# Two loads per chunk of the spectrum instead of three, and a result stored in eight pieces

## The chip, the cores and the metric

The kernel runs on one core of a Trainium2 chip. The metric is the device time of one execution in microseconds (us). A core has a matrix engine (TensorE, PE in the profile, with PEld for its weight loads), three engines for element-wise work (VectorE or DVE, ScalarE or ACT, GpSimd or POOL) and a queue that issues only transfers (SyncE, SP). Transfers (DMAs) can be issued by SP, ScalarE and GpSimd; each tells that it is done through a semaphore. On-chip memory has 128 partitions; matmul results go to a separate memory, PSUM.

## The reference

First a long causal convolution by Fourier transforms, then a mixing over tokens and channels. Batch 8, sequence 5696, 128 channels.

```python
def _attn_ref(x, h):
    B, S, D = x.shape
    L = 2 * S
    Xf = np.fft.rfft(x, n=L, axis=1)
    Hf = np.fft.rfft(h, n=L, axis=0)
    Yf = Xf * Hf[None, :, :]
    y = np.fft.irfft(Yf, n=L, axis=1)[:, :S, :]
    return y.astype(np.float32)

def _moe_ref(x, w_theta, w_tok_r, w_tok_i, w_ch):
    theta = x @ w_theta
    cos_t, sin_t = (np.cos(theta), np.sin(theta))
    zr = x * cos_t
    zi = x * sin_t
    yr = np.einsum('ts,bsd->btd', w_tok_r, zr)
    yi = np.einsum('ts,bsd->btd', w_tok_i, zi)
    y = yr + yi
    u = x + y
    return (u + np.maximum(u @ w_ch, 0.0)).astype(np.float32)
```

The x of the second function is the result of the first.

## The kernel before

**The convolution**, the first 430 us, works in eight groups: two batch rows times one half of the channels (64). The Fourier transform of length 11392 = 178 x 64 is split into matmuls. Stage A (`stage_a`, L248) transforms over the first factor and copies the result to SBUF. Stage B (`stage_b`) goes through the 90 frequencies in 12 chunks of 8 (the last has 2): TensorE does the second factor (`f2`, L268), ScalarE copies the result from PSUM to a tile xs (L417, two buffers), and VectorE multiplies it with the spectrum of h (L419, for the short last chunk L424 twice) into a large tile uv_t. Stage C (L439, L440) and stage D (L475) transform back; stage D's copies (L479, L481) fill a tile yt, 128 partitions (64 channels, two batch rows) by 5696 tokens, of which there is one buffer. PSUM has four buffers that all of these share.

**The spectrum of h** is made once at the start with the same stages (`h_chunk`), its real part in partitions 0 to 63 and its imaginary part in 64 to 127. Its 12 chunks are gathered in the tiles `hst`, which lie in the memory of uv_t, and after every third chunk SP stores three of them to DRAM (`hf_hbm`, L362). The first product of stage B writes over that memory, so it comes after the last of these stores has read it.

In stage B the spectrum comes back chunk by chunk into tiles hs: [128 partitions, 2, 512] in 16 bit, 256 KB. Slot 0 of the middle dimension is the chunk as it lies in DRAM; slot 1 is the same with the two halves of 64 partitions exchanged. L408 loads slot 0, and L410 loads slot 1 in two pieces. There are four buffers hs (`LEAD = 4`): the loads of chunks 0 to 3 are issued during stage C of the group before, and that of chunk c + 4 right after the product of chunk c in the program, so that it waits until that product has freed the buffer.

**The result** of a group is stored to DRAM (`yt_hbm`) by two transfers on SP, one per batch row, 64 partitions by 5696 tokens (L488). For the last group a part goes another way and the rest is issued by GpSimd. The phase steps behind (`phase_step`) read it back, transpose it, take sine and cosine, and store y (L743) and z (L607) on SP; after group 6 SP also copies a part of yt within the chip (L713).

**Order.** The stages of neighbouring groups are woven by hand (`woven`): stage C of group g with stage A of group g + 1, then stage B of group g + 1 with stage D of group g. Below, stage B of "group g" means the products of that group. On TensorE and SP the framework's scheduler sets the order from there. SP takes its queue strictly in that order; an issue that waits holds everything behind it. SP's transfers use eight completion semaphores in turn, and an issue waits until the transfer that used its semaphore before has landed.

**The mixing**, from 430 us on, streams two 5696 x 5696 matrices through TensorE by Strassen-like products (L1266), with GpSimd issuing their loads (L667).

Of the kernel before, what the change touches and what calls it, by code (L numbers as in the profile page):

```python
# [11 lines left out]
BF16 = mybir.dt.bfloat16  # L12
F16 = mybir.dt.float16
# [9 lines left out]
def kernel(  # L23
# [10 lines left out]
    nc = tc.nc  # L34
    B, S, D = x.shape
    assert D == 128
    P = 128
# [28 lines left out]
    H = 22 * P  # L66
# [9 lines left out]
    N2 = 64  # L76
# [3 lines left out]
    CK = 8  # L80
    HD = D // 2
# [6 lines left out]
    NCK = len(CHK)  # L88
    CN = 10
    CHN = [(c0, min(CN, N2 - c0)) for c0 in range(0, N2, CN)]  # L90
    UVW = 2 * HD * K1
    NP = 14
    ND = N2 - 2 * NP
    RC = 2 * NP + 2 * ND
    M0, N0 = S // 4 // N2, S // 4 % N2
    assert S % 4 == 0 and S // 2 == NB // 2 * N2 + N2 // 2 and 2 * NP < N2 // 2
    hf_hbm = nc.dram_tensor("hf_hbm", (NCK, 2, P, HD * CK), F16, kind="Internal").ap()
    yt_hbm = nc.dram_tensor("yt_hbm", (D, B, S), BF16, kind="Internal").ap()

    psp = ExitStack()  # L100
# [2 lines left out]
    def psum():  # L103
        return fp.tile([P, 2, 512], F32, tag="ps", name="ps")

    conv, setup, xa, xin, pha = (ExitStack() for _ in range(5))

    def pool(name, bufs, stack, **kw):
        return stack.enter_context(tc.tile_pool(name=name, bufs=bufs, **kw))

    fa = pool("fft_a", 1, xa)
    fh = pool("fft_h", 4, xa)
    fx = pool("fft_x", 2, xin)
    NE, WB, BT = 9, 6 * 4 * CJ * 64, 7 * 1024
    keep = pool("keep", 1, ctx, side="right")
# [4 lines left out]

    uv_t = fc.tile([P, 2 * UVW + P], F16)
    u_t, v_t = uv_t[:, :UVW + P], uv_t[:, UVW:]
    uv = uv_t[:, :2 * UVW].rearrange("p (r e d k) -> p (r e) d k", r=2, e=2, k=K1)
    a_0 = s1.tile([P, 2 * K1, HD], F16, name="a_0")
# [224 lines left out]
    def h_chunk(c):  # L349
        c0, ck = CHK[c]  # L350
        ps = f2(a_h, c, 0)
        h_ = hst[c // 6][:, c % 6]
        dst = h_[:, :, :, :ck]
        if c in (0, 2, 5, 7, 10):
            nc.vector.tensor_scalar(dst, ps, 16.0 / NF, None, op0=mult)
        else:
            nc.scalar.activation(dst, ps, AF.Copy, scale=16.0 / NF)
        for cc, j in ((0, 0), (NCK - 1, CHK[-1][1] - 1)):
            if c == cc:
                nc.vector.tensor_scalar(dst[:, :, :, j], dst[:, :, :, j], 0.5, None, op0=mult)  # L360
        if c % 3 == 2:
            nc.sync.dma_start(  # L362
                hf_hbm[c - 2:c + 1].rearrange("c h p n -> p (c h) n"),
                hst[c // 6][:, c % 6 - 2:c % 6 + 1].rearrange("p c h d k -> p (c h) (d k)"))

    r_u = fc.tile([P, P], F16)
    r_v = fc.tile([P, RC], F16)
# [27 lines left out]
    def e_minus():  # L395
        nc.gpsimd.tensor_scalar(e_neg[:K1], e_t[:K1, 1:2 * NP:2], -1.0, None, op0=mult)

    LEAD = 4

    def stage_b(a_st, dh, warm=WARM):  # L400

        hs_of = {}

        def load(c):
            if c >= NCK:
                return
            hs = hs_of[c] = fh.tile([P, 2, HD * CK], F16, tag="hs", name="hs")
            nc.sync.dma_start(hs[:, 0], hf_hbm[c, dh])  # L408
            for e in range(2):
                nc.sync.dma_start(hs[64 * e:64 * e + 64, 1], hf_hbm[c, dh, 64 - 64 * e:128 - 64 * e])  # L410

        def chunk(c):
            c0, ck = CHK[c]
            hv = hs_of[c].rearrange("p r (d k) -> p r d k", k=CK)
            ps = f2(a_st, c, warm)
            xs = fs.tile([P, 2, HD, CK], F16, tag="xs", name="xs")
            nc.scalar.activation(xs[:, :, :, :ck], ps, AF.Copy)  # L417
            if ck == CK:
                nc.vector.tensor_tensor(  # L419
                    uv[:, :, :, c0:c0 + ck],  # L420
                    xs.rearrange("p e d k -> p e (d k)").unsqueeze(1).to_broadcast([P, 2, 2, HD * CK]),
                    hv.rearrange("p r d k -> p r (d k)").unsqueeze(2).to_broadcast([P, 2, 2, HD * CK]), op=mult)
            for r in range(2 if ck < CK else 0):
                nc.vector.tensor_tensor(  # L424
                    uv[:, 2 * r:2 * r + 2, :, c0:c0 + ck], xs[:, :, :, :ck],
                    hv[:, r:r + 1, :, :ck].to_broadcast([P, 2, HD, ck]), op=mult)
            load(c + LEAD)
        return [lambda c=c: load(c) for c in range(LEAD)], [lambda c=c: chunk(c) for c in range(NCK)]

# [34 lines left out]
    def stage_d(st, bp, dh, then=None):  # L464
        def chunk(n0, cn):
            if n0 == 0:
                st["yt"] = fy.tile([P, NB, N2], BF16, tag="yt", name="yt")
            g_, yt = st["g"], st["yt"]
            ps = psum()
            nq = 5 if cn == CN else cn  # L470
            for j in range(cn):
                o = ps[:, j // nq, (j % nq) * NB:(j % nq + 1) * NB]
                terms = terms_of(n0 + j)
                for i, (at, e_) in enumerate(terms):
                    nc.tensor.matmul(o, g_[:K1, at, :], e_, start=(i == 0), stop=(i == len(terms) - 1))  # L475
            y_out = yt[:, :, n0:n0 + cn].rearrange("p m (a q) -> p m a q", q=nq)
            y_in = ps[:, :cn // nq, :nq * NB].rearrange("p a (q m) -> p m a q", q=nq)
            if n0 in (0, 3 * CN):
                nc.vector.tensor_copy(y_out, y_in)  # L479
            else:  # L480
                nc.scalar.activation(y_out, y_in, AF.Copy)  # L481
            if n0 + cn == N2:
                if then is not None:
                    then(yt)
                for e in range(2):
                    t0 = H if then else 0
                    with tc.issue_after(sides["row"]) if then else ExitStack():
                        (nc.gpsimd if then else nc.sync).dma_start(  # L488
                            yt_hbm[dh * HD:(dh + 1) * HD, 2 * bp + e, t0:],
                            yt[64 * e:64 * e + 64].rearrange("p m n -> p (m n)")[:, t0:])  # L490
        return [lambda n0=n0, cn=cn: chunk(n0, cn) for n0, cn in CHN]

    zz_n, ZB = [0], 3
# [11 lines left out]
    rr = []  # L505
    r_rest = [lambda: rr.extend([r_table(0, r_u), r_table(1, r_v)]), lambda: rr[0](), lambda: rr[1]()]
    h_chunk(0)
    w2_sine()
    w_rest(1)
    h_chunk(1)  # L510
    w2_cosine()
    for c in range(2, NCK):
        if c == 5:
            w_rest(2)
        h_chunk(c)
        if c in (9, 10):
            a0.pop(0)()
# [19 lines left out]
    def phases_b(ti, y_ap, b0, nb, yT, sb, th_pool, th_tag, zi_eng, turns=None, tags=("red", "mag"), m=P,  # L537
                 theta_ps=None, copy=None, home={}):
        n = nb * D
# [39 lines left out]
        nc.scalar.activation(cos_, mag, AF.Sin, bias=half_pi[:m], scale=-TWO_PI)  # L579
        yflat = y_ap.rearrange("p b d -> p (b d)")  # L580
        if tags is None:
            k = zz_n[0] = (zz_n[0] + 1) % (4 + ZB)
            zz = (fh.tile([P, 2, HD * CK], F16, tag="hs", name="zz").bitcast(BF16) if k < 4 else
                  sides["phases"]["zz"].tile([P, 2, 512], BF16, tag="zz", name="zz"))
            zr, zi = zz[:, 0], zz[:, 1]
            sides["zz"] = zz
        else:
            zi, zr = (z.bitcast(BF16) for z in (sin_, cos_))
# [85 lines left out]
    sides = {"phases": None}  # L674
# [173 lines left out]
    bp = cp = wlp = ybp = None  # L848
# [248 lines left out]
    for i, (k, p, tt, j0, s0, nj) in enumerate(stretches):  # L1097
# [38 lines left out]
        if tt is None:  # L1136
# [24 lines left out]
            if end_of_pair:  # L1161
# [5 lines left out]
                c, c0 = c_last  # L1167
# [161 lines left out]
```

## Time and profile before

| | |
|---|---|
| median of 3 runs | 2084.01 us (2083.17 to 2089.09) |
| the profiled execution | 2084.83 us, span 2083.0 us, mean granted clock 0.978 |
| busy: PE, DVE, ACT, POOL | 1982.1, 1543.9, 639.5, 972.4 us |
| hs loads (SP) | 96 of 128 KB (median 3.1 us to landing), 192 of 64 KB (3.0) |
| spectrum stores (SP) | 4 of 768 KB, 9.0 us |
| result stores (SP) | 14 of 712 KB, 7.7 us; GpSimd 2 of 360 KB |
| first to last start of L419 | 53.2 to 375.1 us |

A row of the groups of instructions reads: line, engine, operation, output <- inputs, shape, count | busy us, mean ns of one | idle us of the engine just before them, and what ended most of it. A row of waits reads: who <- whom: us in total, times, longest. A row of the timeline reads: start us, length us, engine, line, operation, output <- input, count, and in brackets the idle time before it with what ended it. On SP, the length of an issue includes a wait on one semaphore. A row of transfers: count, KB each, median us from issue to landing.

### The profile page before, as it was taken

What the parts mean: (1) busy time and instruction counts of PE and PEld (TensorE: products, weight loads), DVE (VectorE), ACT (ScalarE), POOL (GpSimd) and SP (SyncE); (2) the same over time, 40 slices, a digit from 0 to 9 for tenths busy, and PEclk for the clock granted to TensorE, in tenths of its full rate; (3) what the DMA queues carried; (4) which work ended last, traced back from release to release, by engine and by line L of the source; (5) the groups of instructions that cost most, each with busy time, mean ns of one, the idle gap of its engine ahead of it and who ended that gap; (6) DMA issues with size and microseconds to landing.
All of it is one profiled execution on the core that took longest, in us unless ns stands there. A gap on an engine that the chain in (4) does not pass through costs nothing.

```text
span 2083.0 us, 42942 instructions
## 1 busy us (share of the span) xinstructions
PE 1982.1 (95%) x16381; PEld 1098.0 (53%) x16381; DVE 1543.9 (74%) x2805; ACT 639.5 (31%) x936; POOL 972.4 (47%) x1770
## 2 busy tenths in 40 slices
PE   7698988889999999999999999899999999999998
PEld 5588888754444444444444444344444444444444
DVE  7867767666788787878777766876867777777767
ACT  6667777783333333333310000011111111111111
POOL 8432331247444454445566554445453545444450
PEclk9789999999999999999999999999999999999999
DMA  9699996999898999999999899879697878878793
GB/s 162 97 140 146 157 143 161 240 266 244 147 172 173 178 172 164 175 178 172 179 168 161 131 196 263 132 118 156 119 160 127 154 133 148 144 135 153 129 155 88
DMA packets 518014, 335.08 MB, mean 161 GB/s; under 512 B 186231, under 2 KB 483319, under 8 KB 516823
## 3 DMA queue, kind: packets, MB, share of 16 engines
q0 software_dynamic: 322368, 157.47, 60.0%
q1 hardware_dynamic: 189456, 163.34, 27.7%
q10 hardware_dynamic: 5984, 11.54, 1.6%
q8 instruction: 128, 2.10, 0.4%
q14 instruction: 78, 0.64, 0.1%
HBM read 376.39 MB, written 92.49 MB: 225 GB/s over the span
## 4 chain that ended last, share of the span: by engine, by line
PE 65%; DVE 3%; DMA 3%; issue 1%; POOL 1%; ACT 0%; DVEq 0%; ACTq 0%; SPq 0%
PE m L1266 60%; DVE b L822 1%; DVE c L1273 1%; DMA ring<-in_moe_w_tok_r_dram 1%; PE v L968 1%; PE utp L961 1%; PE m L1270 1%; DMA b<-z_hbm 1%; DVE wt L881 1%; POOL ring L667 1%; PE theta_ps L551 0%; PE tpz L909 0%; DMA wl<-in_moe_w_tok_i_dram 0%; PE m L1187 0%; PE m L1153 0%
## 5 line engine op out<-in xcount | busy, mean ns | idle before, releaser
L667 POOL DMA_DIRECT2D ring<-in_moe_w_tok_i_dram x720 | 387.9, 546 | 651.4 <-DVE wt L881 576.1
L667 POOL DMA_DIRECT2D ring<-in_moe_w_tok_r_dram x720 | 386.5, 547 | 151.0 <-DVE wt L881 82.7
L881 DVE STREAM_TRANSPOSE wt<-ring 128x384 f32<-128x384 f32 (+2 forms) x720 | 360.4, 527 | 120.1 <-PE m L1266 77.5
L1266 PE MATMUL m<-b,wt 128*128 128x512 bf16 x1640 | 390.1, 380 | 1.9 <-DVE wt L881 1.7
L1266 PEld LDWEIGHTS <-wt 128*128 128x128 bf16 x1804 | 176.3, 98 | 219.4 <-DVE wt L881 7.4
L1273 DVE TENSOR_TENSOR c<-c,m 128x512 f32<-128x512 f32 x412 | 266.9, 674 | 0.4 <-PE m L1266 0.4
L963 ACT ACTIVATE ring<-utp 128x512 bf16<-128x512 bf16 x85 | 50.7, 597 | 582.3 <-PE utp L961 582.3
L419 DVE TENSOR_TENSOR uv_t<-xs,hs 128x2048 f16<-128x2048 f16 x88 | 111.6, 1292 | 51.7 <-DMA hs<-hf_hbm 32.4
L439 PE MATMUL ps<-r_u,uv_t 128*128 128x128 f16 x1024 | 123.9, 226 | 16.1 <-DVE uv_t L424 10.9
L440 PE MATMUL ps<-r_v,uv_t 128*128 128x100 f16 x1024 | 121.4, 214 | 1.2 <-DVE uv_t L424 1.0
L1187 PE MATMUL m<-b,wt 128*128 128x512 bf16 x480 | 112.2, 383 | 6.4 <-DMA b<-zz 2.7
L958 ACT ACTIVATE ub<-c 128x512 bf16<-128x512 f32 x88 | 55.0, 628 | 191.8 <-DMA ring<-in_moe_w_tok_r_dram 113.2
L439 PEld LDWEIGHTS <-uv_t 128*128 128x128 f16 x1024 | 104.4, 102 | 12.5 <-DVE uv_t L424 12.1
L151 POOL DMA_DIRECT2D x<-in_x_dram x128 | 99.6, 785 | 22.8 <-POOL x L149 14.7
L440 PEld LDWEIGHTS <-uv_t 128*128 128x128 f16 x1024 | 103.9, 102 | 9.2 <-issue 6.2
L417 ACT ACTIVATE xs<-ps 128x1024 f16<-128x1024 f32 x96 | 91.7, 971 | 48.4 <-DVE uv_t L419 31.6
L1187 PEld LDWEIGHTS <-wt 128*128 128x128 bf16 x528 | 50.9, 99 | 66.4 <-issue 8.7
L268 PEld LDWEIGHTS <-w_t 64*128 64x128 f16 x3240 | 58.3, 99 | 43.8 <-issue 35.7
L553 ACT ACTIVATE red<-theta_ps,magic 128x512 f32<-128x512 f32 (+1 forms) x46 | 31.6, 687 | 155.3 <-PE theta_ps L551 89.4
L248 PE MATMUL ps<-f_t,x 89*128 89x180 f16 x512 | 66.0, 261 | 3.1 <-DVE a L255 1.4
L911 ACT ACTIVATE ring<-tpz 128x512 bf16<-128x512 bf16 (+1 forms) x46 | 27.5, 597 | 131.6 <-PE tpz L909 118.2
L822 DVE TENSOR_TENSOR b<-b 128x1024 bf16<-128x1024 bf16 x100 | 61.4, 684 | 0.0
(2924 smaller groups left out, 3774.6 us busy)
## 6 DMA issues: line engine op xcount, KB each, us to landing
ring<-in_moe_w_tok_r_dram POOLq DMA_DIRECT2D x352, 96.0 KB, 4.5
ring<-in_moe_w_tok_i_dram POOLq DMA_DIRECT2D x352, 96.0 KB, 5.0
ring<-in_moe_w_tok_r_dram POOLq DMA_DIRECT2D x352, 80.0 KB, 4.5
ring<-in_moe_w_tok_i_dram POOLq DMA_DIRECT2D x352, 80.0 KB, 3.9
cp_hbm<-c SPq DMA_DIRECT2D x88, 256.0 KB, 2.5
c<-cp_hbm SPq DMA_DIRECT2D x88, 256.0 KB, 4.3
out_dram<-c SPq DMA_DIRECT2D x88, 256.0 KB, 4.7
hs<-hf_hbm SPq DMA_DIRECT2D x96, 128.0 KB, 3.1
```

The costliest lines, as they stand in the source:

```text
L151: nc.gpsimd.dma_start(x16[p0:p1, e, n0:n0 + 16, :HD], bass.AP(tensor=src.tensor, offset=src.offset + (p0 * N2 + n0) * D + dh * HD, ap=[[N2 ...
L248: nc.tensor.matmul(ps[:, i // 2, (i % 2) * 2 * K1:(i % 2 + 1) * 2 * K1], lhs(q + i), f1_t[:NB], start=True, stop=True)
L417: nc.scalar.activation(xs[:, :, :, :ck], ps, AF.Copy)
L419: nc.vector.tensor_tensor(uv[:, :, :, c0:c0 + ck], xs.rearrange("p e d k -> p e (d k)").unsqueeze(1).to_broadcast([P, 2, 2, HD * CK]), hv. ...
L439: nc.tensor.matmul(o, u_t[:, at:at + P], r_u, start=True, stop=False)
L440: nc.tensor.matmul(o[:, 2 * NP:], v_t[:, at:at + P], r_v, start=False, stop=True)
L667: nc.gpsimd.dma_start(wb[32 * i:32 * i + 32, :ng, :nj * 64], bass.AP(tensor=a.tensor, offset=a.offset + row0 * S + p * H + i * QR + j0 * 6 ...
L822: return [lambda f=f, x=x: f(*x) for f, x in ((nc.vector.tensor_sub, (bt[M3], b12, b22)), (nc.vector.tensor_sub, (bt[M4], b21, b11)), (nc. ...
L881: nc.vector.transpose(wt.rearrange("p j t r -> p (j t r)").bitcast(F32).rearrange("p (j g t) -> p g j t", j=TJ, g=4)[:, :ng, :nj], wb[:, : ...
L1187: nc.tensor.matmul(ms[n // 2 * 2 + h], a[n][:, j, :, r], bts_of[p][jj][n % 2 * 2 + h][:, r, :], start=(n % 2 == 0 and jj == 0 and r == 0), ...
L1266: nc.tensor.matmul(ms[q], a[q][:, j, :, r], bts[jj][q][:, r, :], start=(jj == 0 and r == 0), stop=(jj == NJ - 1 and r == 1 and q not in left))
L1273: nc.vector.tensor_tensor(c, z, ms[q], op=op)
```

## The change

The spectrum lies in DRAM with real and imaginary part side by side for each of 64 rows. Each of the four stores of the spectrum becomes two, one for the real part (partitions 0 to 63) and one for the imaginary part (64 to 127). A chunk's tile hs is then filled by two loads: partitions 0 to 63 take both parts in their order, one run of 2 KB per partition; partitions 64 to 127 take them in reversed order, two runs of 1 KB. The result of each of the first seven groups is stored in four pieces of 1,424 tokens for each of the two batch rows. `LEAD` only moves up and names the number of buffers that was written as 4.

```diff
+    YP = [(n * S // 4, (n + 1) * S // 4) for n in range(4)]
...
-    hf_hbm = nc.dram_tensor("hf_hbm", (NCK, 2, P, HD * CK), F16, kind="Internal").ap()
+    hf_hbm = nc.dram_tensor("hf_hbm", (NCK, 2, N2, 2, HD * CK), F16, kind="Internal").ap()
...
-        if c % 3 == 2:
+        for ri in range(2 if c % 3 == 2 else 0):
             nc.sync.dma_start(
-                hf_hbm[c - 2:c + 1].rearrange("c h p n -> p (c h) n"),
-                hst[c // 6][:, c % 6 - 2:c % 6 + 1].rearrange("p c h d k -> p (c h) (d k)"))
+                hf_hbm[c - 2:c + 1, :, :, ri, :].rearrange("c h p n -> p (c h) n"),
+                hst[c // 6][64 * ri:64 * ri + 64, c % 6 - 2:c % 6 + 1].rearrange("p c h d k -> p (c h) (d k)"))
...
-            nc.sync.dma_start(hs[:, 0], hf_hbm[c, dh])
-            for e in range(2):
-                nc.sync.dma_start(hs[64 * e:64 * e + 64, 1], hf_hbm[c, dh, 64 - 64 * e:128 - 64 * e])
+            nc.sync.dma_start(hs[:64], hf_hbm[c, dh])
+            nc.sync.dma_start(hs[64:], hf_hbm[c, dh, :, ::-1, :])
...
-                for e in range(2):
-                    t0 = H if then else 0
-                    with tc.issue_after(sides["row"]) if then else ExitStack():
-                        (nc.gpsimd if then else nc.sync).dma_start(
-                            yt_hbm[dh * HD:(dh + 1) * HD, 2 * bp + e, t0:],
-                            yt[64 * e:64 * e + 64].rearrange("p m n -> p (m n)")[:, t0:])
+                for t0, t1 in [(H, S)] if then else YP:
+                    for e in range(2):
+                        with tc.issue_after(sides["row"]) if then else ExitStack():
+                            (nc.gpsimd if then else nc.sync).dma_start(
+                                yt_hbm[dh * HD:(dh + 1) * HD, 2 * bp + e, t0:t1],
+                                yt[64 * e:64 * e + 64].rearrange("p m n -> p (m n)")[:, t0:t1])
```

More of the change, by code (lines that the diff above doesn't have):

```diff
@@ L104, in psum @@
         return fp.tile([P, 2, 512], F32, tag="ps", name="ps")
+    LEAD = 4
     conv, setup, xa, xin, pha = (ExitStack() for _ in range(5))
@@ L111 @@
     fa = pool("fft_a", 1, xa)
-    fh = pool("fft_h", 4, xa)
+    fh = pool("fft_h", LEAD, xa)
     fx = pool("fft_x", 2, xin)
@@ L396, in e_minus @@
         nc.gpsimd.tensor_scalar(e_neg[:K1], e_t[:K1, 1:2 * NP:2], -1.0, None, op0=mult)
-    LEAD = 4
     def stage_b(a_st, dh, warm=WARM):
@@ L581, in phases_b @@
         if tags is None:
-            k = zz_n[0] = (zz_n[0] + 1) % (4 + ZB)
-            zz = (fh.tile([P, 2, HD * CK], F16, tag="hs", name="zz").bitcast(BF16) if k < 4 else
+            k = zz_n[0] = (zz_n[0] + 1) % (LEAD + ZB)
+            zz = (fh.tile([P, 2, HD * CK], F16, tag="hs", name="zz").bitcast(BF16) if k < LEAD else
                   sides["phases"]["zz"].tile([P, 2, 512], BF16, tag="zz", name="zz"))
```

## The prediction

> **What bounds the kernel now.** I read the page first. The chain that ended last is for the most part the matmuls of the token mixing after 430 us (60% of the span on L1266), which the change doesn't touch; the change lies in the convolution, the first fifth.
>
> ```profile
> span 2083.0 us, 42942 instructions
> ...
> L419 DVE TENSOR_TENSOR uv_t<-xs,hs 128x2048 f16<-128x2048 f16 x88 | 111.6, 1292 | 51.7 <-DMA hs<-hf_hbm 32.4
> ...
> hs<-hf_hbm SPq DMA_DIRECT2D x96, 128.0 KB, 3.1
> hs<-hf_hbm SPq DMA_DIRECT2D x192, 64.0 KB, 3.0
> ```
>
> VectorE's product with the spectrum (L419) stood idle 51.7 us before its 88 runs, 32.4 of it put down to the loads of hs. Next, the timeline of SP's queue and of VectorE in one stage B, that of group 3 (186 to 207 us):
>
> ```profile
> 188.62 0.33 SPq L408 DMA_DIRECT2D hs<-hf_hbm  x1
> 188.99 1.08 SPq L410 DMA_DIRECT2D hs<-hf_hbm  x2
> ...
> 201.11 0.53 SPq L408 DMA_DIRECT2D hs<-hf_hbm  x1
> 201.69 1.08 SPq L410 DMA_DIRECT2D hs<-hf_hbm  x2
> ```
> ```profile
> 195.21 3.60 DVE L419 TENSOR_TENSOR uv_t<-xs,hs 128x2048 f16<-128x2048 f16 x3 [2.22 <-ACT xs L417]
> ...
> 202.09 2.36 DVE L419 TENSOR_TENSOR uv_t<-xs,hs 128x2048 f16<-128x2048 f16 x2 [1.15 <-ACT xs L417]
> 205.52 1.23 DVE L419 TENSOR_TENSOR uv_t<-xs,hs 128x2048 f16<-128x2048 f16 x1 [1.07 <-DMA hs<-hf_hbm]
> ```
>
> The loads are those of chunks 4 and 10 (that of chunk 8 stands between them, from 197.23), the products those that begin with chunks 4, 8 and 10. A load may start when the product four chunks earlier has freed its buffer. Load 4 starts as product 0 ends, but load 10 starts at 201.11 although product 6 ended at 198.8: SP spends about 1.76 us on each chunk's three issues and is 2.3 us behind. The second row of products says ACT xs, but ScalarE's copies for chunks 4 and 8 were done by 193.0 and 199.9; what was late is the load: the last piece of chunk 8's is issued at 198.35 and lands 3.8 us later, at 202.1. So all three waits, 4.4 us, are the spectrum's. In groups 2 to 6 such waits come to 3.7 to 4.5 us a stage.
>
> What of this the end feels is read on TensorE, in the waits of PE from 140 to 400 us and in the busy time of narrow stretches around two changes of stage (columns: stretch, length, then busy us of PE, PEld, DVE, ACT, POOL; PEclk is the granted clock):
>
> ```profile
> PE ps L439 <- DVE uv_t L424: 10.0, 5, 2.6
> ```
> ```profile
> 163.80:167.20 3.40, 1.80 (x28) 1.50 (x27) 2.01 (x4) 1.54 (x3) 0.00 (x0) 1.00 0.49 141
> 167.20:170.70 3.50, 3.50 (x39) 3.50 (x37) 2.26 (x2) 1.54 (x2) 1.11 (x2) 0.51 0.50 130
> 204.80:208.20 3.40, 1.97 (x29) 1.59 (x26) 1.83 (x3) 2.40 (x5) 0.00 (x0) 1.00 0.43 118
> 208.20:211.60 3.40, 3.40 (x35) 3.40 (x33) 2.30 (x2) 1.25 (x2) 1.11 (x2) 0.50 0.60 150
> ```
>
> Five times, in groups 2 to 6, TensorE has finished stage B and stands 10.0 us in total for VectorE's last product before stage C. Each time the 3.4 us that follow are granted half the clock, and TensorE is busy in all of them, so each costs about 1.7 us more.
>
> Last, the start, SP and then VectorE:
>
> ```profile
> 37.45 0.33 SPq L408 DMA_DIRECT2D hs<-hf_hbm  x1
> ...
> 42.81 0.67 SPq L362 DMA_DIRECT2D hf_hbm<-uv_t  x1
> ```
> ```profile
> 53.19 4.74 DVE L419 TENSOR_TENSOR uv_t<-xs,hs 128x2048 f16<-128x2048 f16 x4 [2.26 <-DMA hs<-hf_hbm]
> ```
>
> The first product overwrites uv_t, which holds the spectrum until its last store has landed. VectorE wrote the last of it by 37.9, but the store stands in SP's queue behind two chunks' loads, is issued at 42.81 and takes 10.2 us, to 53.0. VectorE was free at 50.93.
>
> **The change, part by part.**
>
> *Two loads for three.* 96 of 288 issues go, at 0.53 to 0.59 us. Per chunk SP needs 0.33 to 0.53 plus 0.54, about 1.1 us instead of 1.76, and is no longer behind. It also waits less for its own semaphores: the built program gives SP's DMAs eight in turn, so with three a chunk a load waits for one issued 2.7 chunks before, with two for the load of its own buffer, which has been used. The new sizes, 128 KB into 64 partitions, aren't in the trace. Nearest rows: 64 KB into 64 partitions 3.0 us and 128 KB into 128 partitions 3.1; I take 3.1, since bytes and queue are the same. Bounds: 2.0 (the fastest 128 KB load) and 6.0 (twice the 64 KB row). In group 3 chunk 4 comes 0.54 earlier (one issue less; the landing there, 5.4 us, stays), chunk 8 about 1.2, where ScalarE's copy comes next, and chunk 10 no longer waits. Late next is TensorE's own work, which reaches stage C at 205.8 instead of 207.1.
>
> So for groups 2 to 6 I take TensorE's 10.0 us and leave 0.3 a stage: −8.5. Bounds: 0 (other engines fill the gap) and −22 (five times 4.4). Group 7 has two load waits, 3.02 and 1.64, beside phase work: −2 (0 to −4.7). Group 1 waits 3.29 at chunk 5, mostly on a landing of 5 to 6 us: −1 (0 to −3.3). Half clock: with the wait down to 0.3 the stretch before it is nearly full. How much is enough isn't shown (1.97 of 3.4 isn't); I take two of five away, −3.4 (0 to −8.5).
>
> *Spectrum stores in halves.* Eight issues for four, and in the built order all eight stand ahead of the first load. The last is out near 39 instead of 43, lands near 48 to 49, and product 0 starts when VectorE is free: −2.3. If 384 KB lands no faster than the 768 KB rows (7.4 to 10.2) it is still in time; later than 12 us costs up to 2.3 again. Loads 0 to 3 wait for stores in turn, load 3 lands near 52, needed at 54.5. The rest of group 0's stage has 5.6 us of load waits at landings of 2.3 to 2.4 us: buffers then return every 1.23 + 0.39 + 2.4 = 4.0 us for four chunks, faster than four products (4.9). ScalarE, with the sine tables among its copies, comes next; I take half, −2.7 (0 to −5.6). Group 0 together −5.
>
> *Result in eight pieces.* 42 more issues at 0.57, six in each of seven groups: 3.4 us per group on SP. Behind them stands one load, chunk 3 of the next group, issued by 176.6 now; SP then has nothing until 188.6, which hides the 3.4 us and the wait for the first pieces' semaphores. If that cover were gone it would cost up to 3.4 a group. The landing of 178 KB is between 2.2 (smallest loads) and 7.7; the buffer yt is next written at 189.6, 20 us on. After group 6 there is no such gap: two copies of yt and the y and z stores of the phase steps follow at once (379.8 to 410), and VectorE waits 4.2 us for y stores as it is. Between 0 and +3.4; I take +1.5, since the two whole rows already hold the issues behind them (2.0 us each).
>
> The Trainium skill (DMA: Bandwidth & Descriptors, "Rules for kernel authors") says that two transfers to disjoint partition halves serialize, and that one of 128 partitions is better. The traces of 64 KB halves neither show nor exclude it at 128 KB. By it the sum moves towards the third rival's, by the rows it stays.
>
> *Order elsewhere.* VectorE, ScalarE and GpSimd keep theirs; TensorE moves two and three matmuls inside pieces that aren't finished earlier either way: 0. Packets of the loads fall from 24,576 to 18,432; no price taken.
>
> Sum: −8.5 − 2 − 1 − 3.4 − 5 + 1.5 = −18.4. The profiled execution took 2084.83 us (span 2083.0 and 1.8 around it), so 2066.4; it lies 0.8 over the median 2084.0, so about 2066 as a median.
>
> **Rivals.**
>
> 1. *The gap is filled by others.* Stage B couples three engines (busy 17.2, 15.3 and 16.5 of 21 us), two buffers xs and four in PSUM. If each load wait only turns into one for ScalarE or TensorE, the start's 2.3 and some 2 us remain: 2080. For it: ScalarE's copies wait 31.6 us for L419, so the engines hold each other up already. Against it: TensorE stands idle at every end of B.
> 2. *The clock comes back everywhere.* The stretch at half clock from 54.7 to 75.1 follows TensorE's stop around 51 to 54, which shrinks. All five short stretches gone (5.1 more) and some 5 us there: 2056. The Trainium skill (TensorE: Matmul & The Clock Gate, "Part 1: The HAM clock gate") has a low window of about 3.4 us set the clock to half; the rows above agree, 1.80 busy of 3.4 and then 0.51.
> 3. *Halves land late, slower.* If 128 KB into 64 partitions takes twice the 64 KB row, chunk 4's load (5.5 now) lands 11 us after 189.0, at 200.0 instead of 195.0: +5 in each of seven stages, 2119. It decides once that landing exceeds 6.0, where the issue saved (0.54) is used up. Against it: today's halves land with the 128-partition load at 3.0, with three in flight.
>
> That the change doesn't do what it says I leave out: the built order shows 192 loads and 56 pieces.
>
> **How the numbers follow.** The forecast 0.66 (own range 2060 to 2073), rival 1 0.15, rival 2 0.12, rival 3 0.07. The range runs from rival 2 to rival 1, 2055 to 2080, and leaves out rival 3 and some of both ends. About 0.3% (6 us) can be told from no change, so rival 1 is the same: faster 0.79, same 0.14, slower 0.07.
>
> **What would show it.** SP's loads in pairs about 1.1 us a chunk with no backlog at chunk 10; L419's idle before on hs under 15 us; L439's wait for L424 under 4 us; fewer half-clock stretches at the start of C; the last spectrum store issued before 40 and product 0 near 51; 430 us to the end unchanged. It is wrong if hs loads land over 4 us in the median, if the waits only change name, or if y stores after 380 hold VectorE for far more than 4.2 us.

## The result: 0.9917 of the time before

| | before | after |
|---|---|---|
| median of 4 runs on one chip | 2086.32 us (2083.17 to 2089.09) | 2069.6 us (2066.56 to 2070.24) |
| span of the profiled execution | 2083.0 us | 2068.4 us |

The ratio is 0.9917, 95% interval 0.9897 to 0.9938: faster, by less than the forecast's 18 us but inside its range. In the kernel after, the lines of the code are shifted a little: L418 and L423 are the products with the spectrum, L438 and L439 stage C, L270 the second factor in stage B, L474 stage D, L364 the spectrum stores, L408 and L409 the loads of hs, L487 the result stores, L740 the y store's tile. In the kernels of the experiments they move again by a few lines.

The page of the kernel after (the group of the products, the loads):

```profile
L418 DVE TENSOR_TENSOR uv_t<-xs,hs 128x2048 f16<-128x2048 f16 x88 | 110.6, 1290 | 43.2 <-DMA hs<-hf_hbm 22.8
...
hs<-hf_hbm SPq DMA_DIRECT2D x192, 128.0 KB, 3.6
```

VectorE's idle time before the product fell from 51.7 to 43.2 us, the share put down to hs from 32.4 to 22.8. The load of 128 KB into 64 partitions lands in 3.6 us, against 3.0 to 3.1 for the old ones.

In stage B of group 3, SP's queue of the kernel after (the loads of chunks 8 and 10, then the result stores), and VectorE's products of chunk 4 and of chunks 5 and 6, whose buffers these loads wait for:

```profile
193.46 0.45 SPq L408 DMA_DIRECT2D hs<-hf_hbm  x1
193.94 0.61 SPq L409 DMA_DIRECT2D hs<-hf_hbm  x1
...
196.28 1.50 SPq L408 DMA_DIRECT2D hs<-hf_hbm  x1
197.83 0.60 SPq L409 DMA_DIRECT2D hs<-hf_hbm  x1
...
204.59 5.29 SPq L487 DMA_DIRECT2D yt_hbm<-yt  x8
```
```profile
192.20 1.23 DVE L418 TENSOR_TENSOR uv_t<-xs,hs 128x2048 f16<-128x2048 f16 x1 [1.64 <-DMA hs<-hf_hbm]
193.83 2.36 DVE L418 TENSOR_TENSOR uv_t<-xs,hs 128x2048 f16<-128x2048 f16 x2 [0.40 <-DMA hs<-hf_hbm]
```

Product 4 ends at 193.43 and load 8 is issued at 193.46; product 6 ends at 196.19 and load 10 is issued at 196.28. Where no semaphore holds it (as in the 1.50), SP spends 1.1 to 1.2 us on a chunk; it is not behind. The eight result pieces take 5.29 us of SP's queue; behind them stands one load, chunk 3 of the next group, and then a gap.

The waits of TensorE from 140 to 400 us in the kernel after; the wait that was 10.0 us, five times, is now this line:

```profile
PE ps L438 <- DVE uv_t L423: 0.2, 1, 0.2
```

Stage C therefore no longer starts at half clock: its length falls from between 19.5 and 20.4 us to between 18.03 and 18.05 in groups 2 to 6. But the half clock has not gone from the kernel. TensorE's timeline and two stretches of stage B of group 3, after:

```profile
192.62 1.07 PE L270 MATMUL ps<-a__3541,w_t 64*128 64x64 f16 x61
195.14 0.21 PE L270 MATMUL ps<-a__3541,w_t 64*128 64x64 f16 x3 [1.45 <-issue]
```
```profile
192.20:195.60 3.40, 1.96 (x83) 1.72 (x81) 3.00 (x3) 1.54 (x3) 0.00 (x0) 0.99 0.66 171
195.60:199.00 3.40, 3.40 (x87) 3.27 (x86) 3.40 (x4) 2.97 (x4) 0.00 (x0) 0.51 0.47 134
```

TensorE stops here for 1.45 us for nothing that the profile shows ("issue"), is busy for 1.96 of 3.4 us, and gets half the clock in the next 3.4 us. The same happens in stage B of groups 2, 5 and 7, where 6.8 us each run at half clock.

Where the 14.6 us of span come from, read from the first matmuls of the stages:

| part | before | after | difference |
|---|---|---|---|
| up to stage C of group 0 | 72.23 | 71.32 | −0.9 |
| stage C of group 0, group 1 | 71.54 | 70.99 | −0.6 |
| stage B of groups 2 to 6 (with the wait at its end) | 110.9 | 106.1 | −4.8 |
| stage C of groups 2 to 6 | 99.3 | 90.2 | −9.1 |
| group 7 | 58.43 | 56.51 | −1.9 |
| last stage D and all behind it | 1670.55 | 1673.26 | +2.7 |

In groups 2 to 6 the waits can be told apart from the clock. Stages B and C together took 210.2 us before, 20.5 of them at half clock (from the record of the granted clock); after, 196.3 with 17.1. TensorE is busy in nearly all of the half-clock time, so half of it is lost: 10.2 and 8.6. At full clock that leaves 200.0 and 187.8. So by this estimate the waits gave 12.2 us and the clock 1.7. The profile of the run with the loads alone (below), which has the same code in these stages, gives 8.8 and 3.4: the split is known to some 3 us only. The estimate "sum less half of the half-clock time" is used for the other runs below.

### The profile page after: what moved, and what is told of

The parts are those of the page before. It is cut to its first block, busy times and chain, and to the rows that moved or that the text cites. A ratio compares the mean times of both kernels' runs of the same rounds, so it can differ in the third digit from the quotient of the medians.

```text
span 2068.4 us, 42651 instructions
## 1 busy us (share of the span) xinstructions
PE 1972.6 (95%) x16205; PEld 1097.1 (53%) x16381; DVE 1544.1 (75%) x2805; ACT 640.0 (31%) x936; POOL 975.9 (47%) x1770
## 3 DMA queue, kind: packets, MB, share of 16 engines
q1 hardware_dynamic: 185200, 163.33, 27.3%
## 4 chain that ended last, share of the span: by engine, by line
PE 63%; DVE 3%; DMA 3%; POOL 2%; issue 2%; ACT 0%; DVEq 0%; ACTq 0%; POOLq 0%
PE m L1265 59%; DMA b<-z_hbm 2%; POOL ring L666 1%; DVE c L1272 1%; PE utp L960 1%; PE v L967 1%; PE m L1269 1%; DVE b L821 1%; DVE wt L880 1%; PE m L1152 1%; PE theta_ps L550 0%; PE tpz L908 0%; DMA ring<-in_moe_w_tok_r_dram 0%; DMA ring<-in_moe_w_tok_i_dram 0%; PE m L1186 0%
## 5 line engine op out<-in xcount | busy, mean ns | idle before, releaser
L418 DVE TENSOR_TENSOR uv_t<-xs,hs 128x2048 f16<-128x2048 f16 x88 | 110.6, 1290 | 43.2 <-DMA hs<-hf_hbm 22.8
L438 PE MATMUL ps<-r_u,uv_t 128*128 128x128 f16 x1024 | 116.8, 220 | 6.9 <-ACT g__9008 L443 1.6
L439 PE MATMUL ps<-r_v,uv_t 128*128 128x100 f16 x1024 | 114.4, 208 | 0.4
L153 POOL DMA_DIRECT2D x<-in_x_dram x128 | 98.3, 773 | 20.4 <-POOL x L151 14.6
L439 PEld LDWEIGHTS <-uv_t 128*128 128x128 f16 x1024 | 100.2, 98 | 9.8 <-issue 7.8
L438 PEld LDWEIGHTS <-uv_t 128*128 128x128 f16 x1024 | 100.3, 98 | 1.1 <-DVE uv_t L423 0.7
L270 PEld LDWEIGHTS <-w_t 64*128 64x128 f16 x3240 | 61.3, 102 | 38.6 <-issue 29.5
```

Source lines behind the costliest of these rows:

```text
L153: nc.gpsimd.dma_start(x16[p0:p1, e, n0:n0 + 16, :HD], bass.AP(tensor=src.tensor, offset=src.offset + (p0 * N2 + n0) * D + dh * HD, ap=[[N2 ...
L418: nc.vector.tensor_tensor(uv[:, :, :, c0:c0 + ck], xs.rearrange("p e d k -> p e (d k)").unsqueeze(1).to_broadcast([P, 2, 2, HD * CK]), hv. ...
L438: nc.tensor.matmul(o, u_t[:, at:at + P], r_u, start=True, stop=False)
L439: nc.tensor.matmul(o[:, 2 * NP:], v_t[:, at:at + P], r_v, start=False, stop=True)
```

## The experiments

Twelve kernels were run, in four sets with the kernel before on the same chip. Times are medians; each ratio is against the kernel before of the same set.

**Loads alone, pieces alone.** The first is the kernel after with whole rows stored, the second the kernel before with the eight pieces.

```diff
-    YP = [(n * S // 4, (n + 1) * S // 4) for n in range(4)]
+    YP = [(0, S)]
```

> The changed kernel with the results stored in two whole rows again (two loads per chunk and the spectrum's stores in halves stay). Theory: the two loads per chunk carry the whole gain and the pieces nothing, so about 2069 us, stages B and C as in the changed kernel (C of groups 2 to 6 at 18.0 us), and SP's two stores at about 1.2 us. Rival: the pieces carry part of it, because whole rows hold up the other transfers; then stage C is back at 19.5 to 20.4 us and the time at 2075 to 2080.

> The kernel before with the results stored in eight pieces (three loads per chunk stay). Theory: 2084 to 2087 us, no difference outside noise; at most 3 us slower from the phase steps, where SP's y stores come later. Stage C of groups 2 to 6 stays at 19.5 to 20.4 us and the first product at 53.2. Rival: the pieces shorten stage C; then C near 18 us and the time near 2077.

Loads alone: 2069.65 us, ratio 0.9928 (0.9913 to 0.9944). Pieces alone: 2085.17 us, 0.9992 (0.9979 to 1.0005). The gain is the loads', and the pieces are worth nothing that can be told. The waits for y stores, of which the forecast made a cost of the pieces, do not go with them. VectorE's waits between 360 and 450 us in the kernel after, then with the loads alone, then with the pieces alone:

```profile
DVE ring L740 <- DMA y_hbm<-ring: 8.3, 7, 3.9
```
```profile
DVE ring L740 <- DMA y_hbm<-ring: 5.5, 5, 2.7
```
```profile
DVE ring L742 <- DMA y_hbm<-ring: 3.1, 3, 1.2
```

They were 4.2 before: with three loads a chunk the pieces go with shorter waits (3.1), with two with longer ones (8.3 against 5.5).

**Count of loads or layout.** The kernel after with its layout in DRAM and its pieces, but the first load of a chunk split in two, so three loads again.

```diff
-            nc.sync.dma_start(hs[:64], hf_hbm[c, dh])
+            for r in range(2):
+                nc.sync.dma_start(hs[:64, r], hf_hbm[c, dh, :, r])
             nc.sync.dma_start(hs[64:], hf_hbm[c, dh, :, ::-1, :])
```

> The changed kernel with the first of a chunk's two loads split in its two slots, so three loads again (64, 64 and 128 KB), with the new layout, the same bytes, the spectrum's stores in halves and the results in eight pieces. Theory: what gained was SP's share (one issue and one semaphore turn less per chunk), so the gain goes: 2080 to 2087 us, stage B of groups 2 to 6 at 21.5 to 23 us and SP at 1.7 us or more a chunk. Rival: the new layout (longer runs, fewer packets) gained; then it stays at 2068 to 2073 us.

2096.08 us, ratio 1.0042 (1.0028 to 1.0056): the whole gain is lost and a little more, beyond the expected 2080 to 2087. The group of the products and SP's queue in a stage B of this kernel:

```profile
L419 DVE TENSOR_TENSOR uv_t<-xs,hs 128x2048 f16<-128x2048 f16 x88 | 112.0, 1292 | 64.0 <-DMA hs<-hf_hbm 43.3 <-ACT xs L417 17.3 <-ACT yt L481 1.8
```
```profile
197.49 1.78 SPq L409 DMA_DIRECT2D hs<-hf_hbm  x2
199.32 0.60 SPq L410 DMA_DIRECT2D hs<-hf_hbm  x1
200.02 1.19 SPq L409 DMA_DIRECT2D hs<-hf_hbm  x2
201.25 0.60 SPq L410 DMA_DIRECT2D hs<-hf_hbm  x1
```

SP issues without a pause, about 2.2 us a chunk (the next begins at 201.95), and VectorE waits 43.3 us for hs. These loads land in 2.8 to 3.0 us, faster than the 3.6 of the kernel after. So it is not the landing and not the layout that made the kernel after faster, it is one load less per chunk on a queue that had become the pace of the stage. Why a chunk costs SP 2.2 us here and not 1.76 as in the kernel before was not tested. TensorE's wait before stage C is back with 14.5 us, and so is the half clock behind it.

**The half clock at the start of stage C.** The kernel before, with twelve matmuls of no use at the start of stage C (128 x 384, into a PSUM tile that stage C then overwrites) which keep TensorE busy while it waits.

```diff
             ps = psum()
+            if q == 0:
+                idle(ps, 12, w_t2[:, 2:5].rearrange("p k n -> p (k n)"), 384)
```

> The kernel before with twelve matmuls of 128x384 ahead of the first matmul of each stage C, into a PSUM tile that stage C then overwrites; they need nothing from stage B, so TensorE does them while it waits for VectorE's last product. Theory: the half-clock stretch at the start of stage C comes from that wait, so with it filled the stretch goes and C of groups 2 to 6 falls by 1.5 to 2.0 us each to about 18.0 from its own first matmul, while the fill (1.9 us against waits of 1.35 to 2.63) costs up to 0.5 us each: 2076 to 2081 us. Rival: stage C was longer for another reason (transfers or late loads at its start); then C stays at 19.5 to 20.4 and the time at 2085 or above.

2083.42 us, ratio 0.999 (0.9977 to 1.0003). Stage C did fall, to 17.8 to 18.4 us, but stage B grew to 22.0 to 25.4, and groups 2 to 6 together took 208.9 us instead of 210.2. The half-clock time in them is 20.5 us, as before; it has moved into stage B. This is the longest stretch, in group 4 of this kernel:

```profile
232.70:242.90 10.20, 9.80 (x227) 8.93 (x224) 6.38 (x6) 5.91 (x7) 0.00 (x0) 0.50 0.74 142
```

Ahead of it stands a stop of 1.58 us for "issue". The expected gain was not there: a stop that no longer costs the clock in one place was followed by one that did in another.

**What the loads left are worth.** The kernel after without the loads of chunks 4 to 11; their products use the tile that chunk c − 4 left, so the result is not the reference's.

```diff
         def load(c):
...
+            if c >= LEAD:
+                hs_of[c] = hs_of[c - LEAD]
+                return
```

> The changed kernel with the loads of chunks 4 to 11 left out: these chunks multiply with the spectrum of chunk c modulo 4 that is already there, so the result isn't the reference's. Theory: what is left of stage B's length are still the load waits (chunk 4 above all) and the half-clock stretches that TensorE's stops in them bring, so B of groups 2 to 6 falls to 19.0 to 19.5 us from 19.3 to 23.0, and the time to 2057 to 2063 us. Rival: the waits only change their name, because ScalarE and TensorE are as late; then B stays within 0.5 us of the changed kernel in each group and the time at 2066 to 2070.

2053.44 us, ratio 0.9847 (0.9832 to 0.9862): by the two ratios some 15 us under the kernel after, and below the expected 2057 to 2063. Its group of products, with hs gone from the waits:

```profile
L421 DVE TENSOR_TENSOR uv_t<-xs,hs 128x2048 f16<-128x2048 f16 x88 | 110.6, 1291 | 27.4 <-ACT xs L419 26.1 <-DMA hs<-hf_hbm 1.0
```

Groups 2 to 6 take 185.8 us and none of it at half clock. Set against 187.8 for the kernel after once its half-clock loss is taken out, the remaining loads cost only 2 us there; the other 8.6 of the 10.5 us are the clock. By the profile of the loads alone it is 5.4 and 6.9 of 12.3. Up to stage C of group 0 this kernel is 3.2 us earlier.

**The x loads.** While stage B runs, GpSimd loads the next x. Three variants of the kernel after: those of later groups are allowed to start earlier (first diff), those of group 1 are held until stage A of group 0 is done (second), and both.

```diff
-                nc.gpsimd.tensor_copy(x16[0:1, e, n0, 0:1], g_[0:1, 0, 16 * i:16 * i + 1])
+                nc.gpsimd.tensor_copy(x16[0:1, e, n0, 0:1], g_[0:1, 0, 8 * i:8 * i + 1])
```
```diff
-    for f in load_x(1):
-        f()
+    x_late = load_x(1)
...
+    nc.gpsimd.tensor_copy(x16s[1][0:1, 0, 0, 0:1], a_0[0:1, 0, HD - 1:HD])
+    for f in x_late:
+        f()
```

> The changed kernel with the loads of x for the group after next released twice as early within stage C (piece i after the copy of column 8 i instead of 16 i). Theory: the load of chunk 4 takes 5 us or more to land because the last x loads still run when stage B begins; with x done earlier it lands in 3 to 4 us, its wait (0.8 to 1.7 us a stage) goes, and TensorE's stop and the half-clock stretch in stage B go with it in some groups: 2060 to 2066 us. Rival: the landing is long for another reason, or the x loads, denser now, hold up stage C's start: 2068 to 2074 us.

> The changed kernel with the loads of x for group 1 held back until stage A of group 0 is done (near 46 us). Theory: the eight spectrum stores take 13 to 15 us to issue and the last lands near 54 because they share the transfer engines with those x loads; without them the stores are out by 40 and landed by 48, and the first product starts at 46 to 50 instead of 54.4; the end moves by less, 0 to 5 us earlier, or later if stage A of group 1 then waits for x. Rival: SP's issue of the stores is slow by itself; then they still take 13 us and the first product stays at 53 to 55.

> The two changes to the x loads together. Theory: their gains add, 2056 to 2064 us. Rival: 2068 or above, if either costs elsewhere.

Earlier x loads: 2068.25 us, ratio 0.9905 (0.989 to 0.9919), not to be told from the kernel after. The waits that this was to remove did go: VectorE's waits for hs in groups 2 to 6 fell from 9.4 to 0.3 us. But those for ScalarE's copies rose from 14.8 to 23.6, so the time is the rival's. Held x loads: 2076.71 us, 0.9948 (0.9935 to 0.996). Both: 2076.8 us, 0.9952 (0.994 to 0.9964), the rival's 2068 or above. The held loads do show what the start waits for. SP's spectrum stores in the kernel after, VectorE's first products, and the stores again with the x loads held:

```profile
30.74 14.76 SPq L364 DMA_DIRECT2D hf_hbm<-uv_t  x8
45.60 1.72 SPq L408 DMA_DIRECT2D hs<-hf_hbm  x1
```
```profile
54.35 4.74 DVE L418 TENSOR_TENSOR uv_t<-xs,hs 128x2048 f16<-128x2048 f16 x4 [4.70 <-DMA hs<-hf_hbm]
```
```profile
30.93 11.10 SPq L363 DMA_DIRECT2D hf_hbm<-uv_t  x8
```

With the x loads out of the way the eight issues take 11.1 instead of 14.8 us from first to last, 8.5 instead of 13.0 without the pauses between them; the last store lands at 46.0 instead of 53.5, and the first product starts at 50.08 instead of 54.35. What the x loads take is seen in the 24 us from 30 to 54 us of the kernel before, of the kernel after and of this one (the last two columns are the share of the 16 DMA engines' time, over 1 where packets overlap, and GB/s):

```profile
30.00:54.00 24.00, 16.20 (x450) 14.36 (x443) 16.07 (x27) 14.05 (x20) 14.43 (x18) 0.93 1.49 230
30.00:54.00 24.00, 19.01 (x482) 16.54 (x476) 17.59 (x27) 14.82 (x20) 15.16 (x20) 0.79 1.49 226
30.00:54.00 24.00, 20.75 (x502) 18.35 (x496) 19.57 (x31) 17.29 (x23) 8.88 (x12) 0.72 0.90 193
```

Before and after, the DMA engines are equally full and move nearly the same amount; only with x held is there room. So the stores are slow while x comes in. They are not quick without it either: four of the eight issues still take 1.3 to 2.0 us. The variant loses all the same: stage A of group 1 then waits for its x, and stage C of group 0 starts at 80.60 instead of 71.32.

**Spectrum loads that wait for no product.** If the remaining waits are the turn of the four buffers, more memory should remove them. In groups 0 to 6 the tile of the group's own x is used up when stage B begins; chunks 4 to 11 are put there. The first kernel does this on the kernel after, the second on the kernel before (three loads, whole rows).

```diff
-            hs = hs_of[c] = fh.tile([P, 2, HD * CK], F16, tag="hs", name="hs")
+            if c < LEAD or g + 1 == B:
+                hs = hs_of[c] = fh.tile([P, 2, HD * CK], F16, tag="hs", name="hs")
+            else:
+                hs = hs_of[c] = x16s[g].rearrange("p e n d -> p (e n d)")[
+                    :, (c - LEAD) * 2 * HD * CK:(c - LEAD + 1) * 2 * HD * CK].rearrange("p (r n) -> p r n", r=2)
...
-            load(c + LEAD)
+            if g + 1 == B:
+                load(c + LEAD)
+            elif c < LEAD:
+                load(LEAD + 2 * c)
+                load(LEAD + 2 * c + 1)
```

> The changed kernel, but in groups 0 to 6 the spectrum chunks 4 to 11 are loaded into memory of their own (the tile of this group's x, which stage A has used up by then) and not into the buffers that products 0 to 7 free; two are issued behind each of the first four products. Theory (what is left of VectorE's waits for the spectrum is the turn of the four buffers plus a landing of 3.6 to 5 us): loads of chunks 4 to 11 wait for no product, L418's idle on hs falls from 22.8 to under 10 us, stage B of groups 2 to 6 falls from 19.3 to 23.0 us toward the 18.5 to 20.1 of the run without these loads, no half clock inside stage B, and the time is 2053 to 2060. Rival (landings at the head of stage B, 5 us beside the x loads, are what is left): chunks 4 and 5 still come late, and the time is 2062 to 2069.

> The same memory for chunks 4 to 11, but on the kernel before, with three loads a chunk and whole rows stored. Theory (the count of loads matters through SP: 1.76 us a chunk, and it stays even where no buffer is awaited): SP issues eight chunks in about 14 us and stays ahead of products that come every 1.8 us only by a little, so some waits stay; 2062 to 2078, above the run with two loads. Rival (buffers were all that mattered, and SP's queue only because it stood behind them): equal to the run with two loads within 3 us.

Two loads: 2083.55 us, ratio 0.9986 (0.9971 to 1.0). Three loads: 2074.44 us, 0.9944 (0.9922 to 0.9965). Both expectations of the first run were wrong: it gave back nearly all of the gain. The second lies within its theory's numbers, but not above the run with two loads as that theory said. VectorE's waits for the spectrum did go, to 4.5 us between 0 and 440 us and to nothing in groups 2 to 6; there it waits 43.5 us for ScalarE's copies instead. But now 16 loads go out in a row (in group 3 from 177.2 to 191.9), beside the x loads and from ahead of stage B on, and TensorE stops. TensorE's timeline in group 3 of the first kernel, two stretches, and the transfers by queue from 182.6 to 183.0 us (packets, MB, share of the 16 engines' time):

```profile
181.98 0.99 PE L270 MATMUL ps<-a__3517,w_t 64*128 64x64 f16 x55
185.62 0.30 PE L270 MATMUL ps<-a__3517,w_t 64*128 64x64 f16 x9 [2.65 <-issue]
```
```profile
183.00:185.00 2.00, 0.00 (x0) 0.00 (x0) 2.00 (x3) 1.02 (x1) 0.00 (x0) 1.00 1.59 212
187.20:190.60 3.40, 3.40 (x67) 3.18 (x65) 1.83 (x2) 1.94 (x2) 0.00 (x0) 0.50 0.89 190
```
```profile
q0 software_dynamic: 247, 0.03, 118.6%
q1 hardware_dynamic: 35, 0.04, 35.7%
q8 instruction: 1, 0.02, 16.6%
```

TensorE stands for 2.65 us for "issue" and then gets half the clock; in groups 2 to 6 the stops are 2.08 to 2.77 us, one in each, and 54.6 us run at half clock. The third fence is a hint at what the stop waits for. Queue q8 moves 128 pieces of 16 KB in the whole run (2.1 MB in the page), and TensorE has some 32,600 matmuls and weight loads in the trace, so one piece stands for some 255 of them, an inference from these two counts. Between 138 and 360 us, TensorE stops for "issue" for over 1.4 us once in the kernel before, four times in the kernel after, five times in this one and six times in each of the two that follow: in all 22 a transfer of q8 stands 2.0 to 3.2 us ahead of the end of the stop. In the traces of all 14 kernels there are 49 such stops, and the transfer stands 2.3 to 3.9 us ahead of each end; since 35 to 40 such transfers fall into these 222 us, one in some 6 us, chance would not put one there every time. In stage B TensorE runs 64 and then 30 matmuls, each with its weight load, in 1.11 and 1.42 us at full clock, so 255 instructions take some 3.4 us, hardly more than that delay. That TensorE waits there for its own code is therefore what the traces point to; no run changed that supply alone. Why some pieces come too late is not shown: the share of the DMA engines around the stop is 1.59 here, but only 0.66 around that of the kernel after, shown above.

**At once, or the held x tile.** Two more kernels were to tell whether the 16 loads at once cost the time, or that the x tile stays taken until the last product, so that later x loads begin after stage B. The first puts only chunks 4, 5, 10 and 11 into the tile and runs six chunks ahead; the second keeps the order of the kernel after and puts only chunks 10 and 11 there.

```diff
-            if c < LEAD or g + 1 == B:
+            if c not in (4, 5, 10, 11) or g + 1 == B:
...
-            elif c < LEAD:
-                load(LEAD + 2 * c)
-                load(LEAD + 2 * c + 1)
+            elif c == 0:
+                for i in range(3):
+                    load(LEAD + i)
+            elif c < 6:
+                load(c + 6)
```
```diff
-            if c < LEAD or g + 1 == B:
+            if c < 10 or g + 1 == B:
...
-            if g + 1 == B:
-                load(c + LEAD)
-            elif c < LEAD:
-                load(LEAD + 2 * c)
-                load(LEAD + 2 * c + 1)
+            load(c + LEAD)
```

> The changed kernel, but in groups 0 to 6 only the spectrum chunks 4, 5, 10 and 11 lie in memory of their own (the tile of this group's x); chunks 6 to 9 take the four buffers as products 0 to 3 free them, and the loads run six chunks ahead instead of four. The tile of x is held until the last product, as in the run with eight chunks in it, but only two chunks are loaded at once at the head of stage B. Theory (in the run with eight chunks the 16 loads at once, which landed in 6.9 us, were what cost): stage B of groups 2 to 6 goes below that of the changed kernel, to 19 to 21 us, and the time is 2054 to 2066. Rival (what cost there is that the next x loads start only after the last product): stage B stays at 23 to 26 us and the time is 2076 to 2086.

> The changed kernel with its loads four chunks ahead, but chunks 10 and 11 of groups 0 to 6 lie in the tile of this group's x, so that this tile is held until the last product and the x loads that reuse it start after stage B; the loads of the spectrum are paced as in the changed kernel. Theory (loads at once were what cost): within 4 us of the changed kernel, 2065 to 2072. Rival (the held tile costs): 2076 to 2086.

Six ahead: 2084.11 us, ratio 0.9992 (0.9978 to 1.0007). Held tile: 2076.0 us, 0.9954 (0.9941 to 0.9967). Both theories that named the loads at once fall, and the numbers are those of the rival, the second at its very edge. It is not proven by that, since the scheduler issued the four loads of chunks 10 and 11 ahead of chunk 4's, at the head of stage B, as this part of SP's queue in the second kernel shows:

```profile
215.28 0.46 SPq L412 DMA_DIRECT2D x<-hf_hbm  x1
...
217.23 0.60 SPq L413 DMA_DIRECT2D x<-hf_hbm  x1
221.00 0.44 SPq L412 DMA_DIRECT2D hs<-hf_hbm  x1
```

So a few early loads and the held tile both remain as a cause of the later code, and no kernel here separates them. What is measured is where the time is. Groups 2 to 6 in all runs (us):

| kernel | B + C | at half clock | less half of that |
|---|---|---|---|
| before | 210.2 | 20.5 | 200.0 |
| pieces alone | 212.9 | 23.9 | 201.0 |
| idle matmuls | 208.9 | 20.5 | 198.7 |
| three loads, new layout | 220.1 | 30.7 | 204.7 |
| after | 196.3 | 17.1 | 187.8 |
| loads alone | 198.1 | 13.7 | 191.2 |
| x loads earlier | 195.5 | 10.2 | 190.4 |
| x loads of group 1 held | 203.7 | 20.5 | 193.5 |
| both | 203.2 | 20.5 | 193.0 |
| 8 chunks in the x tile, two loads | 215.6 | 54.6 | 188.3 |
| 8 chunks in the x tile, three loads | 206.1 | 27.3 | 192.4 |
| 4 chunks in it, six ahead | 211.7 | 44.4 | 189.5 |
| 2 chunks in it | 207.0 | 34.1 | 190.0 |
| no loads of chunks 4 to 11 | 185.8 | 0.0 | 185.8 |

The last column has two levels. Where the loads of hs keep up it is 186 to 194, whatever the buffers; where SP issues three a chunk into four buffers, 199 to 205. Inside a level, differences of 3 us come with the same code (after, loads alone). The estimate takes TensorE as busy in all of the half-clock time; by the traces it is in 81 to 100% of it, in the kernel with both changes to x in 73%. By it, the rest of the differences is half-clock time. Of the variants with all loads none was faster than the kernel after beyond what the measurement can tell.

## Why the prediction was right, and where it was not

- **SP's queue, as forecast.** 1.1 to 1.2 us a chunk, no backlog at chunk 10, and TensorE's wait before stage C down from 10.0 to 0.2 us. The run with three loads shows that the count of loads is the cause.
- **Groups 2 to 6: the sum near, its split not decided.** Forecast −8.5 for the waits and −3.4 for the clock, −11.9; by the kernel after −12.2 and −1.7, −13.9; by the loads alone −8.8 and −3.4, −12.2. The forecast took only TensorE's 10.0 us. Between 140 and 400 us of the kernel after its waits for stage D's copies shrank too, from 9.2 to 4.5, while its stops for "issue" in stage B grew from 5.4 to 8.0.
- **The half clock: right place, wrong consequence.** "I take two of five away": in fact all five went from stage C, which alone gave 9.1 us. But stage B got 17.1 us of half clock instead of 3.4. The forecast treated the half clock as part of the stop that it removed. It follows other stops of that size too, and stage B has some. Rival 2, in which the clock comes back everywhere, fell by this, although the five short stretches that it named did go; the half clock of the first 76 us, of which it expected some 5 us, grew from 23.9 to 27.3. The Trainium skill (TensorE: Matmul & The Clock Gate, "Part 1: The HAM clock gate") has the clock set by how busy a window of about 3.4 us was, wherever it lies; the stretch with 1.96 busy of 3.40 and 0.51 behind it, now inside stage B, agrees.
- **Rival 1**, waits that only change name, was half true: L418 still waits 22.8 us for hs and 19.3 for ScalarE, where "under 15" for hs was forecast. At full clock little of it counts: the run without those loads has only 2 to 5 us less, and with earlier x loads the waits for hs became waits for ScalarE at the same time.
- **The start: the step that failed.** Forecast −5 for group 0, measured −0.7 (−0.9 up to its stage C, +0.2 in it); this is rough, since up to that stage C single profiles of the same code differ by 2 us (69.4 with x loads earlier, 69.9 with the loads alone, 71.3 after). "The last is out near 39 instead of 43, lands near 48 to 49": eight issues took 14.8 us, to 45.5, the last was issued at 43.4 and landed at 53.5, and the load of chunk 0, now behind all eight, at 54.2; the first product came at 54.35 instead of 53.19. What failed first is the price of an issue. The forecast had the last two stores out about 1 us after VectorE's last write at 37.9, and the trace gave no warning: in the kernel before even the four stores of 768 KB took SP only 0.36 to 0.67 us each, with loads or pauses between them. Eight in a row took 0.6 to 0.7 for the first three and 2.1 to 2.3 for each of the others. And the forecast reckoned with the order of SP's queue alone: the DMA engines were as full from 30 to 54 us as they are now (1.49), so an earlier place in the queue was no earlier landing. So the halves gave nothing there where −2.3 was taken. That they cost 1.2 us is not shown: in the eight kernels with halves and x loads not held the first product starts at 51.8 to 54.4, in the four with whole stores at 53.0 to 53.2. The rest of stage B made up some 2 us, near the −2.7 taken for it.
- **Group 7 and group 1** came as forecast: −1.9 for −2, −0.7 for −1 (with the loads alone group 7 has only −0.9).
- **The pieces.** Nothing in stage B, as forecast. The +1.5 behind stage D measured as +2.7, but that is no proof of the step: loads alone have −1.2 there (1669.32), pieces alone +1.1 (1671.6), and VectorE's wait for y stores is longest where both are in. One sign of being wrong did come, "if y stores after 380 hold VectorE for far more than 4.2 us": it is 8.3. As a whole the pieces can't be told from nothing.
- **Rival 3**, halves that land late, is out: 3.6 us in the median, and at the head of stage B, where a load takes over 5 us, it did so before too (chunk 4 of group 3: 5.4 to 5.6 before, 4.6 to 5.4 after). The Trainium skill (DMA: Bandwidth & Descriptors, "Rules for kernel authors") has two transfers to disjoint halves of the partitions serialize; 3.6 us against 3.0 to 3.1 leaves no room for the doubling that rival 3 made of it. Whether one transfer of 128 partitions would be better still, no run here shows.

The forecast of 2066 against 2069.6 thus stands on the right mechanism. By the profiled executions the terms differ by +4.3 at the start, +1.2 behind the last stage D, −2.0 in groups 2 to 6 and +0.4 in groups 1 and 7, together +3.8 with rounding (−14.6 for −18.4). That the miss at the start stays small in the end is partly luck: the excess in groups 2 to 6 makes up for half of it.

## What to carry to other kernels

Where a queue issues for a stage whose buffers return one by one, compare its issue time per step with the pace of the stage before anything about bytes: 1.76 us an hs chunk held up a stage of 1.8 us a chunk, 1.2 us did not; and 1.76 did less harm (192.4 for 200.0) where most loads waited for no buffer. A price of an issue read where issues stand apart need not hold for eight in a row; where the DMA engines are full, look at their share before you count on an earlier landing. And when a stop of TensorE is removed, do not book the half clock behind it as gain until the next stop is known; separate the two in the result by the granted clock.

## What was not expected of the hardware

- The half clock moves. Keeping TensorE busy ahead of stage C left the half-clock time of groups 2 to 6 at 20.5 us; it came back behind stops of 1.2 to 1.6 us in stage B, two for "issue" and one for a copy of ScalarE.
- Stops of 1.4 to 4.1 us that wait for nothing in the program, each of the 49 between 138 and 360 us with a 16 KB transfer of instructions 2.3 to 3.9 us ahead of its end. In the run without the loads of chunks 4 to 11 none over 0.94 us occurs in groups 2 to 6; with 16 loads at once there is one in each.
- Not each such stop costs the clock: with earlier x loads one of 2.17 us did not.
- Eight stores of 384 KB in a row take 13.0 us of issues while x is loaded and 8.5 us when it is held back, a single issue up to 2.3 us; four of 768 KB with loads or pauses between them took 0.36 to 0.67 us each.
